# One crossbar transpose per token tile in place of two, in an attention kernel followed by a two-layer network

## Chip, cores, metric

One core of a Trainium2 chip. The metric is the device time of the kernel in microseconds, median of several executions. "PE" is TensorE, "DVE" VectorE, "ACT" ScalarE, "POOL" GpSimd and "SP" SyncE in the profile.

## The reference

```python
# q, k, v: (4 batches, 8 heads, 768 positions, 64); three of the heads are "retrieval" heads
scores = q @ k.T / 8
mask   = causal, and for the other heads: 4 sink positions or a window of 64
a      = softmax(scores masked);  attn = a @ v
x      = attn as (3072 tokens, 512)
h      = x @ w_in                # 512 -> 2048
out    = (h - tanh(h)) @ w_out   # 2048 -> 512, float32
```

## The kernel before

Tokens are worked on in 12 tiles of 256 (two blocks of 128, `NB = 2`). A small scheduler in Python (`Plan`) gets every operation with an assumed duration, its inputs and outputs, plays the engines through, and emits the instructions in the order that it finds. From tile 3 on ("ranked" tiles) the attention output `x16t` of a tile is transposed by DMA into `xT`; in tiles 0 to 2 PE transposes it and DVE or ACT copies it into `xT`. The first layer then reads `xT`:

```python
def st_X_tile(t):
    xTs[t] = lazy(xt_pool, [128, HP, TT], FP16, "xT", f"xT{t}")      # HP = 4, TT = 256
    for i in range(NB):
        op("SP", 1250,                                               # assumed ns of issue
           lambda i=i: nc.sync.dma_start_transpose(
               out=xTs[t]()[:, :, i * 128 : i * 128 + 128],
               in_=x16s[t]()[:, i, :, :].rearrange("p h d -> p (h d)")),
           r=[("x16t", t)], w=[("xT", t, "all", i)], dma=(512, 22.0))  # packets, ns each
# ... first layer of a tile, two blocks of 128 features a unit
nc.tensor.matmul(out=ph()[:, j, :], lhsT=w()[:, cb, c0 + fb % 4 : c0 + 512 : 4],
                 rhs=xTs[t]()[:, cb, :], start=(cb == 0), stop=(cb == HP - 1))
# ... a finished block of 128 tokens is stored
op(ring, 420, lambda: engs[ring].dma_start(out=out[t0:t0+128, c0:c1], in_=ot()[:, c0:c1]), ...)
# ... the whole is followed by a branch to a second version of the program, not taken with these inputs
program(True)
with tc.If(many[0] > NGEN, preferred_fallthrough_block=True, label="redo"):
    program(False)
```

SyncE issues nearly all loads of q, k and v, all transposes by DMA and all stores but one. Each of its transfers, when it has landed, signals a semaphore (a counter on which an engine can wait).

The softmax here doesn't subtract the row's maximum and nothing guards it: scores larger than these inputs give would overflow.

Of the kernel before, what the change touches and what calls it, by code (L numbers as in the profile page):

```python
# [8 lines left out]
FP16 = mybir.dt.float16  # L9
# [3 lines left out]
TT = 256  # L13
NB = TT // 128


class Plan:
# [42 lines left out]
    def run(self, fill=None, until=None):  # L60
        self.fill = fill
        n = len(self.ops)
        users = [[] for _ in range(n)]
        followers = [[] for _ in range(n)]
        left = [0] * n
        for i, o in enumerate(self.ops):
            left[i] = len(o[3]) + (o[7] is not None)
            for d in o[3]:
                users[d].append(i)
            if o[7] is not None:  # L70
                followers[o[7]].append(i)
        ready = [0.0] * n
        free = dict.fromkeys(self.ENGINES, 800.0)
        queue = {e: [] for e in self.ENGINES}
        rings = {"SP": [], "POOL": []}
        now = 0.0
        self.start = [0.0] * n
        self.done = [0.0] * n
        order = []

        self.port = 0.0

        def at(i):

            return max(ready[i], self.port) if self.ops[i][6] else ready[i]

        def enqueue(i):
            queue[self.ops[i][0]].append(i)

        def finish(i, done):  # L90
            self.done[i] = done
            e, ns = self.ops[i][:2]
            for u in users[i]:
                to = self.ops[u][0]
                if to == e and e == "PE":
                    at = self.start[i] + ns
                else:
                    at = done + (60 if to == "PE" else 40)
                ready[u] = max(ready[u], at)
                left[u] -= 1  # L100
                if not left[u]:
                    enqueue(u)

        for i in range(n):
            if not left[i]:
                enqueue(i)
        while len(order) < n:
            t, e = min(
                [(max(free[e], min(at(i) for i in q)), e) for e, q in queue.items() if q],
                default=(1e12, None),  # L110
            )

            live = [r for r in rings.values() if r and r[0][1] <= now]
            nxt = min([r[0][1] for r in rings.values() if r and r[0][1] > now], default=1e12)
            if live:
                pk = sum(r[0][2] for r in live)
                end, r = min((now + r[0][3] * pk / r[0][2], k) for k, r in enumerate(live))
                stop = min(end, nxt, t)
                for x in live:
                    x[0][3] -= (stop - now) * x[0][2] / pk  # L120
                now = stop
                if end <= min(nxt, t):
                    i = live[r].pop(0)[0]
                    finish(i, now + 1300)
                    continue
                if nxt < t:
                    continue
            elif nxt < t:
                now = nxt
                continue  # L130
            now = max(now, t)
            i = min(
                (i for i in queue[e] if at(i) <= t), key=lambda i: self.ops[i][5]
            )
            queue[e].remove(i)
            _, ns, _, _, dma, _, port, _ = self.ops[i]
            if e == "PE" and t < 5600:
                ns *= 2
            self.start[i] = t
            order.append(i)  # L140
            free[e] = t + max(ns - self.OVERLAP[e], 40)
            if port:
                self.port = free[e]
            for u in followers[i]:
                ready[u] = max(ready[u], free[e])
                left[u] -= 1
                if not left[u]:
                    enqueue(u)
            if dma:
                packets, each = dma  # L150
                rings["POOL" if e == "POOL" else "SP"].append(
                    [i, t + ns + (1200 if e == "POOL" else 1000 if t < 6000 else 400), each, packets * each / 16]
                )
            else:
                finish(i, t + ns + self.RESULT[e])
        self.end = max(self.done)
        free = self.FROM
        for i in order:
            if self.ops[i][0] == "PE":
                idle = self.start[i] - free  # L160
                if self.fill and idle > 200 and i != until and self.FROM < free:
                    self.fill(int(idle * 0.5 / 107), 256)
                free = max(free, self.start[i] + self.ops[i][1])
                if i == until:
                    self.fill = None
            self.ops[i][2]()
# [3 lines left out]
def kernel(  # L170
# [98 lines left out]
    def program(first):  # L269
# [19 lines left out]
        def lazy(pl, shape, dt, tag, name):  # L289
            box = []  # L290

            def get():
                if not box:
                    box.append(pl.tile(shape, dt, tag=tag, name=name))
                return box[0]

            return get
# [813 lines left out]

        def st_X_tile(t):

            xTs[t] = lazy(xt_pool, [128, HP, TT], FP16, "xT", f"xT{t}")
            for i in range(NB):
                op(
                    "SP", 1250,
                    lambda i=i: nc.sync.dma_start_transpose(
                        out=xTs[t]()[:, :, i * 128 : i * 128 + 128],
                        in_=x16s[t]()[:, i, :, :].rearrange("p h d -> p (h d)"),  # L1120
                    ),
                    r=[("x16t", t)], w=[("xT", t, "all", i)], dma=(512, 22.0),
                )

        def x_keys(t):
            if ranked(t):
                return [("xT", t, "all", i) for i in range(NB)]
            return [("xT", t, c) for c in range(HP)]

        def st_X(n, tag="m", eng="DVE"):  # L1130
            t, hp = divmod(n, HP)
            if hp == 0:
                xTs[t] = lazy(xt_pool, [128, HP, TT], FP16, "xT", f"xT{t}")
            xp, key = bank([128, NB, 128], FP16, tag, f"xp{n}")

            def mm():
                for i in range(NB):
                    nc.tensor.transpose(
                        out=xp()[:, i, :], in_=x16s[-1 - n]()[:, i, :, :], identity=ident16[:]
                    )  # L1140

            first_x.append(op("PE", 112, mm, r=[("x16", n), "ident"], w=[key]))
            op(
                eng, {"ACT": 373, "DVE": 290}[eng],
                lambda: copy(eng, xTs[t]()[:, hp, :], xp()[:].rearrange("p i c -> p (i c)")),
                r=[key], w=[("xT", t, hp)],
            )

# [6 lines left out]
        def H_unit(t, u):  # L1155
            if u == 0:
                gts[t] = lazy(g_pool, [128, NFB, TT], FP16, "gt", f"gt{t}")
            ph, key = bank([128, FU, TT], FP32, "h", f"ph{t}_{u}")
            for j in range(FU):

                def mm(j=j):
                    fb = u * FU + j
                    w, c0 = w_in_t[fb // 4]
                    for cb in range(HP):
                        nc.tensor.matmul(  # L1165
                            out=ph()[:, j, :], lhsT=w()[:, cb, c0 + fb % 4 : c0 + 512 : 4],
                            rhs=xTs[t]()[:, cb, :], start=(cb == 0), stop=(cb == HP - 1),
                        )

                op(  # L1170
                    "PE", 4 * 109, mm,
                    r=[("win", u * FU // 4)] + x_keys(t), w=[key],
                )
            th = lazy(th_pool, [128, FU, TT], FP32, "th", f"th{t}_{u}")
            tk = ("th", t * NFU + u)
            op(
                "ACT", 597,
                lambda: nc.scalar.activation(  # L1178
                    out=th()[:], in_=ph()[:], func=AF.Tanh, scale=1.0 / XS
                ),  # L1180
                r=[key], w=[tk],
            )
            op(
                "DVE", 687,
                lambda: nc.vector.scalar_tensor_tensor(  # L1185
                    out=gts[t]()[:, u * FU : (u + 1) * FU, :], in0=th()[:], scalar=-XS,
                    in1=ph()[:], op0=ALU.mult, op1=ALU.add,
                ),
                r=[key, tk], w=[("gt", t, u)],
            )  # L1190
# [287 lines left out]
```

## Time and profile before

| | before |
|---|---|
| median (runs) | 237.61 us (237.30 to 237.75) |
| span of the profiled execution | 235.8 us |
| PE busy, 80 to 230 us | 150.0 of 150 us |
| start of the last matmul, from the trace | 229.84 us |
| transfers issued by SyncE, from the trace | 127 |

The rows are from two views of the kernel before, SyncE's instructions of line 1441 (the end of the branch) and of line 1473 (the end of the program); the columns are least, median and greatest duration in ns, then the first and the last start in us.

```profile
L1441 SPq EVENT_SEMAPHORE  x8: 17/17/17, 233.0 to 233.5; - x8
...
L1473 SPq EVENT_SEMAPHORE  x14: 17/28/28, 233.6 to 235.7; - x14
L1473 SPq DRAIN  x3: 7/7/136, 234.8 to 235.2; - x3
```

Eight waits, one for each of the semaphores of its transfers, stand one after the other and take 17 ns each; but each starts 0.07 to 0.1 us after the one before. They begin at 233.0 us, when the last store has landed, and only when all eight are through does the closing sequence of line 1473 begin.

### The profile page before, as it was taken

The numbers are of one execution on the slowest core, as the hardware profiler recorded it, in microseconds if no ns is written. First come the engines' busy times: TensorE is split into PE (matmuls) and PEld (weight loads), VectorE is DVE, ScalarE is ACT, GpSimd is POOL, SyncE is SP. The second block draws the span as 40 slices with busy tenths as digits, with TensorE's granted clock in tenths as the row PEclk, the third lists the DMA queues.
The fourth block names the chain that finished last, engine by engine and source line by source line (L and its number), as shares of the span: only waits on it lengthen the run. The fifth ranks groups of instructions, "written<-read, shape, count | busy, mean of one in ns | idle before, by whom it ended". The sixth has DMA issues, their size and how long they took to land. (4 is left out here: it accounts for less than half of the span.)

```text
span 235.8 us, 5930 instructions
## 1 busy us (share of the span) xinstructions
PE 223.4 (95%) x2234; PEld 158.4 (67%) x2234; DVE 138.9 (59%) x343; ACT 143.2 (61%) x221; POOL 90.2 (38%) x218
## 2 busy tenths in 40 slices
PE   6888899999999999999999999999999999999990
PEld 2455687766675787677777767767677677777660
DVE  3657667862688468658675647567576555434400
ACT  3886749883676498547668458456856754444410
POOL 5798250198709087570904829144000000000000
PEclk9999999999999999999999999999999999999997
DMA  5999999999899999979998995987302101410021
GB/s 129 266 199 207 194 187 219 216 244 204 111 220 189 230 232 184 232 175 191 204 193 199 181 230 121 200 187 141 86 3 81 37 19 47 90 44 26 21 101 41
DMA packets 106084, 35.83 MB, mean 152 GB/s; under 512 B 96195, under 2 KB 102595, under 8 KB 106051
## 3 DMA queue, kind: packets, MB, share of 16 engines
q1 hardware_dynamic: 94754, 30.03, 62.6%
q0 software_dynamic: 11008, 5.24, 16.8%
q8 instruction: 18, 0.29, 0.6%
q10 hardware_dynamic: 288, 0.14, 0.2%
q14 instruction: 16, 0.12, 0.2%
HBM read 27.27 MB, written 6.29 MB: 142 GB/s over the span
## 5 line engine op out<-in xcount | busy, mean ns | idle before, releaser
L1165 PE MATMUL ph<-xT,win 128*128 128x256 f16 x768 | 100.7, 273 | 1.6 <-DMA win<-in_moe_w_in_dram 0.6
L1224 PE MATMUL po<-wout,gt 128*128 128x512 f16 (+1 forms) x400 | 97.4, 371 | 0.3 <-ACT ot L1200 0.3
L1185 DVE SCALAR_TENSOR_TENSOR gt<-th,ph 128x512 f16<-128x512 f32 x96 | 65.6, 685 | 50.1 <-ACT th L1178 49.6
L1178 ACT ACTIVATE th<-ph 128x512 f32<-128x512 f32 x96 | 57.6, 601 | 60.8 <-PE ph L1165 56.4
L1165 PEld LDWEIGHTS <-win 128*128 128x128 f16 x768 | 80.6, 114 | 14.4 <-issue 2.2
L991 ACT ACTIVATE pt<-sc 128x1024 f16<-128x1024 f32 (+1 forms) x78 | 68.6, 927 | 8.8 <-PE sc L971 8.5
L1224 PEld LDWEIGHTS <-gt 128*128 128x128 f16 x400 | 36.4, 98 | 25.5 <-issue 1.0
L709 POOL CAST t<-raw_rqk 128x256 f16 x72 | 28.9, 439 | 56.1 <-DMA raw_rqk<-in_k_dram 47.6
L1060 PEld LDWEIGHTS <-pt 128*128 128x128 f16 x552 | 25.1, 97 | 9.8 <-DVE pt L1021 0.7
L1060 PE MATMUL av<-v,pt 128*128 128x65 f16 x304 | 25.5, 193 | 0.2 <-DVE pt L1021 0.2
L704 POOL CAST v<-raw_rv 128x128 f16 x72 | 21.8, 335 | 4.0 <-DMA raw_rv<-in_v_dram 4.0
L971 PE MATMUL sc<-qk 64*128 64x128 f16 (+1 forms) x412 | 23.1, 236 | 0.0
L1090 DVE TENSOR_TENSOR x16t<-av,rinv 128x128 f32 x72 | 20.8, 289 | 2.0 <-DVE rinv L1080 0.2
L1200 ACT ACTIVATE ot<-po 128x512 f32<-128x512 f32 (+1 forms) x24 | 14.3, 594 | 10.7 <-PE po L1224 10.0
L971 PEld LDWEIGHTS <-qk 64*128 64x128 f16 x412 | 13.6, 94 | 9.7 <-issue 6.7
L1060 PE MATMUL av<-vf,pt 128*128 128x65 f16 x248 | 19.6, 193 | 0.0
L1080 DVE RECIPROCAL rinv<-av 128x4 f32<-128x4 f32 x48 | 8.6, 179 | 11.3 <-PE av L1060 11.1
L1016 DVE TENSOR_TENSOR pt<-pt,mS 128x512 f16<-128x512 f16 x24 | 10.4, 473 | 7.7 <-ACT pt L991 7.7
L1026 DVE TENSOR_TENSOR pt<-pt,m 128x1024 f16<-128x1024 f16 x16 | 11.8, 737 | 4.4 <-ACT pt L991 4.4
L780 POOL TENSOR_TENSOR vf<-v,rflagr 128x260 f16<-128x260 f16 x12 | 7.7, 643 | 0.0
L872 PEld LDWEIGHTS <-t 128*128 128x128 f16 x48 | 3.2, 97 | 5.9 <-ACT t L673 2.4
L459 PE MATMUL warm<-ones 128*128 128x512 f16 (+1 forms) x14 | 4.7, 487 | 1.2 <-POOL ones L454 1.2
(98 smaller groups left out, 95.4 us busy)
## 6 DMA issues: line engine op xcount, KB each, us to landing
out_dram<-ot SPq DMA_DIRECT2D x23, 256.0 KB, 2.8
raw_rqk<-in_q_dram SPq DMA_DIRECT2D x22, 256.0 KB, 4.8
raw_rqk<-in_k_dram SPq DMA_DIRECT2D x22, 256.0 KB, 4.7
raw_rv<-in_v_dram SPq DMA_DIRECT2D x18, 256.0 KB, 5.0
win<-in_moe_w_in_dram POOLq DMA_DIRECT2D x4, 512.0 KB, 9.8
wout<-in_moe_w_out_dram POOLq DMA_DIRECT2D x4, 512.0 KB, 11.7
raw_rv<-in_v_dram SPq DMA_DIRECT2D x4, 128.0 KB, 4.7
v<-in_v_dram POOLq DMA_DIRECT2D x4, 128.0 KB, 9.3
```

Source lines behind the costliest of these rows:

```text
L704: nc.gpsimd.tensor_copy(out=v1s[b]()[:, lo : lo + NB, rank : rank + 1, 0:D], in_=raw_of("v", t)[:, :, at, :],)
L709: nc.gpsimd.tensor_copy(out=t16[t % 2][:, :, :, rank : rank + 1, :], in_=raws["rqk", t][0]()[:, :, :, at, :],)
L971: nc.tensor.matmul(out=sc()[:, hh, o : o + nb * 128].rearrange("p (i c) -> p i c", c=128), lhsT=ks.rearrange("p i c -> p (i c)")[p_, jb * ...
L991: lambda pt=pt, gi=gi, wid=wid, sc=sc: nc.scalar.activation(out=pt()[:, :, 512 * gi : 512 * gi + wid], in_=sc()[:, :, 0:wid], func=AF.Exp, ...
L1026: nc.vector.tensor_mul(out=pv, in0=pv, in1=m4[:, h0 : h0 + 2, 256:512].unsqueeze(2).to_broadcast([128, 2, 2, 256]),)
L1060: nc.tensor.matmul(out=av()[:, i, hh, :], lhsT=pt()[:, hh, co : co + 128], rhs=vv, start=(jb == first_jb), stop=(jb == qb),)
L1090: nc.vector.tensor_mul(out=x16s[t]()[:, :, at, :], in0=av()[:, :, hh : hh + 1, 0:D], in1=rinv()[:, :, hh : hh + 1].unsqueeze(3).to_broadca ...
L1165: nc.tensor.matmul(out=ph()[:, j, :], lhsT=w()[:, cb, c0 + fb % 4 : c0 + 512 : 4], rhs=xTs[t]()[:, cb, :], start=(cb == 0), stop=(cb == HP ...
L1178: lambda: nc.scalar.activation(out=th()[:], in_=ph()[:], func=AF.Tanh, scale=1.0 / XS),
L1185: lambda: nc.vector.scalar_tensor_tensor(out=gts[t]()[:, u * FU : (u + 1) * FU, :], in0=th()[:], scalar=-XS, in1=ph()[:], op0=ALU.mult, op ...
L1200: nc.scalar.activation(out=ot()[:, c0:c1], in_=po()[:, c0:c1], func=AF.Copy, scale=1.0 / XS)
L1224: nc.tensor.matmul(out=po()[:, c0:c1], lhsT=gts[t]()[:, f, ts * 128 : ts * 128 + 128], rhs=w_out_t[f // 4]()[:, f % 4, c0:c1], start=(f == ...
```

## The change

The intent: one transfer of 1024 columns a tile in place of two of 512, so nine transfers fewer in SyncE's queue. For that `xT` lies in order of token blocks, and its readers and writers follow.

```diff
-            xTs[t] = lazy(xt_pool, [128, HP, TT], FP16, "xT", f"xT{t}")
-            for i in range(NB):
-                op("SP", 1250,
-                    lambda i=i: nc.sync.dma_start_transpose(
-                        out=xTs[t]()[:, :, i * 128 : i * 128 + 128],
-                        in_=x16s[t]()[:, i, :, :].rearrange("p h d -> p (h d)")),
-                    r=[("x16t", t)], w=[("xT", t, "all", i)], dma=(512, 22.0))
+            xTs[t] = lazy(xt_pool, [128, NB, HP, 128], FP16, "xT", f"xT{t}")
+            op("SP", 1250,
+                lambda: nc.sync.dma_start_transpose(
+                    out=xTs[t]()[:].rearrange("p i c k -> p (i c) k"),
+                    in_=x16s[t]()[:].rearrange("p i h d -> p (i h d)")),
+                r=[("x16t", t)], w=[("xT", t, "all")], dma=(1024, 22.0))
 ... tiles 0 to 2
-                lambda: copy(eng, xTs[t]()[:, hp, :], xp()[:].rearrange("p i c -> p (i c)")),
+                lambda: copy(eng, xTs[t]()[:, :, hp, :], xp()[:]),
 ... first layer
-                            out=ph()[:, j, :], ...
-                            rhs=xTs[t]()[:, cb, :], ...
+                            out=ph()[:, j, :].rearrange("p (i k) -> p i k", i=NB), ...
+                            rhs=xTs[t]()[:, :, cb, :], ...
```

(Lines are joined. Left out are the list of keys for which the readers of `xT` wait, which follows the change, and a rewriting of one assumed latency that leaves its value as it was.)

More of the change, by code (lines that the diff above doesn't have):

```diff
@@ L151, in run @@
                 rings["POOL" if e == "POOL" else "SP"].append(
-                    [i, t + ns + (1200 if e == "POOL" else 1000 if t < 6000 else 400), each, packets * each / 16]
+                    [i, t + ns + (1200 if e == "POOL" and t < 12000 else 1200 if e == "POOL" else 1000 if t < 6000 else 400), each, packets * each / 16]
                 )
@@ L1112, in st_X_tile @@
         def st_X_tile(t):
-            xTs[t] = lazy(xt_pool, [128, HP, TT], FP16, "xT", f"xT{t}")
-            for i in range(NB):
-                op(
-                    "SP", 1250,
-                    lambda i=i: nc.sync.dma_start_transpose(
-                        out=xTs[t]()[:, :, i * 128 : i * 128 + 128],
-                        in_=x16s[t]()[:, i, :, :].rearrange("p h d -> p (h d)"),
-                    ),
-                    r=[("x16t", t)], w=[("xT", t, "all", i)], dma=(512, 22.0),
-                )
+            xTs[t] = lazy(xt_pool, [128, NB, HP, 128], FP16, "xT", f"xT{t}")
+            op(
+                "SP", 1250,
+                lambda: nc.sync.dma_start_transpose(
+                    out=xTs[t]()[:].rearrange("p i c k -> p (i c) k"),
+                    in_=x16s[t]()[:].rearrange("p i h d -> p (i h d)"),
+                ),
+                r=[("x16t", t)], w=[("xT", t, "all")], dma=(1024, 22.0),
+            )
         def x_keys(t):
             if ranked(t):
-                return [("xT", t, "all", i) for i in range(NB)]
+                return [("xT", t, "all")]
             return [("xT", t, c) for c in range(HP)]
@@ L1132, in st_X @@
             if hp == 0:
-                xTs[t] = lazy(xt_pool, [128, HP, TT], FP16, "xT", f"xT{t}")
+                xTs[t] = lazy(xt_pool, [128, NB, HP, 128], FP16, "xT", f"xT{t}")
             xp, key = bank([128, NB, 128], FP16, tag, f"xp{n}")
@@ L1165, in mm @@
                         nc.tensor.matmul(
-                            out=ph()[:, j, :], lhsT=w()[:, cb, c0 + fb % 4 : c0 + 512 : 4],
-                            rhs=xTs[t]()[:, cb, :], start=(cb == 0), stop=(cb == HP - 1),
+                            out=ph()[:, j, :].rearrange("p (i k) -> p i k", i=NB),
+                            lhsT=w()[:, cb, c0 + fb % 4 : c0 + 512 : 4],
+                            rhs=xTs[t]()[:, :, cb, :], start=(cb == 0), stop=(cb == HP - 1),
                         )
```

## The prediction

> **What bounds the kernel now.** The median of three runs is 237.61 us (237.30 to 237.75); the profiled execution spans 235.8 us. I first read the busy shares and the 40 slices of the page.
>
> ```profile
> PE 223.4 (95%) x2234; PEld 158.4 (67%) x2234; DVE 138.9 (59%) x343; ACT 143.2 (61%) x221; POOL 90.2 (38%) x218
> ...
> PE   6888899999999999999999999999999999999990
> PEclk9999999999999999999999999999999999999997
> DMA  5999999999899999979998995987302101410021
> ```
>
> TensorE is busy in every slice but the first few and the last, at a full granted clock. The DMA engines are nearly full too, but only to slice 27 (about 160 us). Busy ends of matmuls are modelled, so I asked for the busy time by stretch.
>
> ```profile
> 0.00:40.00 40.00, 34.31 (x355) 23.04 (x356) 24.66 (x74) 27.67 (x48) 23.48 (x42) 1.00 1.29 198
> 40.00:80.00 40.00, 38.94 (x443) 26.96 (x441) 26.84 (x74) 26.55 (x40) 22.18 (x59) 1.00 1.17 203
> 80.00:230.00 150.00, 150.00 (x1442) 108.40 (x1439) 86.97 (x197) 88.97 (x134) 44.52 (x117) 1.00 0.60 131
> 230.00:236.00 6.00, 0.11 (x2) 0.00 (x0) 0.42 (x1) 0.00 (x0) 0.00 (x0) 0.76 0.10 33
> ```
>
> The columns after the length of the stretch are PE, weight load, VectorE, ScalarE and GpSimd. From 80 to 230 us PE has no idle time that the trace shows; before 40 us it has 5.7 us, between 40 and 80 us 1.1 us, and the tail of 6 us is the last store. To see hidden stalls I took the distances between the starts of neighbouring matmuls in the trace from 40 to 230 us. A matmul of the first layer (256 columns) is followed by its like after a median of 109 ns (577 cases, at most 138), one of 512 columns after 216 ns (272 cases, at most 228). So PE streams. What is left over those steps: each visit to the score matmuls costs 96 ns on entry (205 ns in place of 109 from a first-layer matmul) and about 95 ns on leaving (148 in place of 53). That is a fixed price of switching, about 31 visits, 5.9 us. True waits after 70 us I count as four, 1.4 us together. PE's own wait list from 60 us on is this:
>
> ```profile
> PE ph L1165 <- DMA xT<-x16t: 0.4, 1, 0.4
> PE po L1224 <- ACT ot L1200: 0.3, 1, 0.3
> PE av L1060 <- DVE pt L1021: 0.2, 1, 0.2
> ```
>
> One of them, once, is for the transposed x that the change touches. It is tile 3, the first that is transposed by DMA:
>
> ```profile
> 72.09 2.53 SPq L1118 DMA_TRANSPOSE xT<-x16t  x2
> 74.67 1.48 SPq L342 DMA_DIRECT2D raw_rqk<-in_k_dram  x1
> ...
> 77.35 0.22 PE L1060 MATMUL av<-v,pt 128*128 128x65 f16 x2
> 77.93 1.50 PE L1165 MATMUL ph<-xT,win 128*128 128x256 f16 x12 [0.36 <-DMA xT<-x16t]
> ```
>
> By the landing semaphores the two halves landed at 77.24 and 77.89 us, and the matmul began at 77.93. For the other eight tiles the second half landed ahead of the first matmul that reads it by 4.9, 1.9, 7.8, 10.7, 2.8, 10.8, 9.3 and 4.7 us (tiles 4 to 11, from the same semaphores and the matmuls' starts). So the transposes are off the critical path but for half a microsecond.
>
> **What the Trainium skill says.** (1) "DMA: Bandwidth & Descriptors", Rules for kernel authors: small transfers should be coalesced into large ones, and under Issuing engines are not separate DMA queues, all of them run on the same 16 engines, so issue is a sequencer cost. The trace agrees on the issue side: a transpose of half the size costs as much to issue. (2) Same page, Latency and other measured facts: a DMA transpose gets 261 GB/s with a non-contiguous middle dimension and about 350 to 400 GB/s contiguous. The new destination is contiguous within a partition, the old one is not; for 256 KB that is, as an estimate from this page, 1.0 against about 0.7 us. The trace can't confirm it: loads run beside the transposes. (3) "TensorE: Matmul & The Clock Gate", Back-to-back issue gap: 256 columns take 262 cycles and 512 take 518 when warm; the 109 and 216 ns above agree.
>
> **The change part by part.**
>
> ```profile
> L1118 SPq DMA_TRANSPOSE xT<-x16t x18: 1189/1244/3186, 72.1 to 201.3; - x18
> ...
> DMA to landing us min/median/max: 2.3/2.7/5.2
> ...
> L727 SPq DMA_TRANSPOSE qk<-t x18: 1244/1324/2774, 52.6 to 160.7; - x18
> ...
> DMA to landing us min/median/max: 3.0/3.8/5.0
> ```
>
> The numbers are least, median and greatest issue time in ns; the second pair are the transposes of q and k, which have just the size of the new one (128 partitions by 1024 columns, where the old one had 512).
>
> *Removed:* nine transposes. 18 issues by 1244 ns = 22.4 us of SyncE become nine of 1244 to 1324 ns = 11.2 to 11.9 us. SyncE's queue is 10.5 to 11.2 us shorter, 1.2 us a tile. No engine's busy time has it, and PE waits for SyncE in one place only, so on the path it is worth at most that wait.
>
> *Moved, the transposed x's arrival:* before, the second half is issued 1.24 us after the first and lands 2.7 us later, 3.9 us in all; after, one issue lands in 3.8 us (the q and k row). A saving of 0.1 us in the usual case, for eight tiles hidden behind at least 1.9 us. For tile 3 the rings were backlogged: the first half needed 5.15 us, and the second, issued 1.27 us later, came 0.65 us after it. Both were queued by 74.6 us, so the same packets should end at about the same 77.9 us; if the contiguous destination helps, 0.3 us sooner. Worth 0 to 0.3 us there, and never more than the stall: from the last attention matmul, which normally occupies 29 ns, to the first-layer one is 550 ns, so 0.5 us.
>
> *Moved, loads behind it:* each goes out about 1.2 us earlier up to 160 us. They feed GpSimd's casts, which wait for q and k in 34.2 us of the stretch after 60 us, and still PE waits for none of it. Off the path: 0.
>
> *Added, the layout that PE reads:* the 576 first-layer matmuls of the nine tiles, and the 192 of the three others, read 256 columns as two runs of 128 elements, 1 KB apart. If a run's end cost even 5 ns, 768 would be 3.8 us, the largest number in this sum. Against it: the mask matmuls already read two runs of 256 and follow each other after 215 ns, just like 512 contiguous columns (216); the score matmuls read 256 columns in two runs with gaps between them, at a 105 to 117 ns step where they are not paired. So I take 0.
>
> *Added, twelve copies into the new layout* for tiles 0 to 2: the copies into q and k's tile already write two runs of 128 with a gap, in 288 ns on VectorE against 289 for x, and 388 against 377 ns on ScalarE. At most 8 by 11 ns = 0.1 us, on engines that are not the bound.
>
> *Moved, the order of the program:* the kernel's instructions are ordered by a small scheduler in Python that assumes times. With one transpose it believes x to be ready earlier: issue 1250 + 400 + 1024 packets by 22 ns over 16 engines (1408) + 1300 = 4358 ns, where two gave 2500 + 400 + 704 + 1300 = 4904 ns. So from tile 3 on it may place first-layer matmuls up to 0.55 us earlier in PE's queue, and everything after can fall differently. The earlier part is unchanged.
>
> Sum on the path: tile 3's wait 0 to -0.5 us, mostly 0.2; layout 0; reordering of unknown sign, of the order of a half microsecond. That gives 237.6 - 0.2 = 237.4 us.
>
> **Rivals.** *Reordering makes new stalls.* For it: the believed gain of 0.55 us a tile is not real (0.1 us by the trace), so the wait of tile 3 can grow from 0.5 to 1.0 us. Against it: for the other tiles the believed 4.4 us still exceeds the usual 3.8. It would make 237.9 to 238.3 us. *Reordering helps:* if two visits to the score matmuls merge, 0.19 us each; three merged, with tile 3's wait gone, 236.5 us. All of the true waits after 70 us gone is 1.4 us: 236.2 us, about the floor. *PE pays for the two runs:* 5 ns each, 241.4 us, still only 1.6%; the mask matmuls speak against it. *SyncE was the bound after all:* 11 us fewer of issue would then show as several per cent, as the 47 us of GpSimd's waits for loads suggest; PE's 150 busy of 150 us speaks plainly against it.
>
> **Range and chances.** The runs before spread over 0.45 us. With -0.5 to +0.5 us of reordering on top of the central -0.2 us, 236.5 to 238.2 us should hold it 8 times in 10. Two per cent is 4.75 us, more than all true waits of PE after 40 us and more than the layout's cost at 5 ns a matmul, so within 2% gets 0.97; slower gets 0.02 for a layout cost that the mask matmuls don't show, faster 0.01.
>
> **What would show it.** Right: nine issues of x's transpose at 1.2 to 1.3 us, landing in 3 to 4 us; first-layer matmuls still 109 ns apart; PE still 150 busy in 150 us; PE's wait for the transposed x at most 1 us, once. Wrong: steps above 112 ns in the first layer (the layout costs); several PE waits for the transposed x (the scheduler was misled); an issue of over 2 us (one large transpose is no cheaper than two); or an end of PE's stream that moved by over 1.5 us with none of these, which would mean that the visits to the score matmuls changed in number.

## The result, and the profile after

| | before | after |
|---|---|---|
| median of 4 runs each | 237.46 us (237.10 to 237.75) | 236.14 us (236.09 to 236.29) |
| ratio | | 0.9946, interval 0.9929 to 0.9964 |
| span of the profiled execution | 235.8 us | 234.5 us |
| last matmul starts | 229.84 us | 229.41 us |
| last store landed | 232.98 us | 232.75 us |
| from its landing to the span's end | 2.78 us | 1.71 us |
| transfers issued by SyncE | 127 | 118 |

Ratios here and below are not quite the ratio of the medians quoted; the range in brackets after a ratio is its 95% interval.

It is within 2%, as forecast, but 0.36 us below the range. The page of the changed kernel, its slices and the stretches:

```profile
PE 223.7 (95%) x2234; PEld 158.4 (68%) x2234; DVE 138.5 (59%) x343; ACT 143.3 (61%) x221; POOL 87.6 (37%) x218
...
PE   7888899999999999999999999999999999999991
```

```profile
40.00:80.00 40.00, 39.14 (x445) 27.12 (x443) 27.09 (x75) 26.79 (x41) 22.11 (x59) 1.00 1.13 204
80.00:230.00 150.00, 149.68 (x1439) 108.17 (x1437) 86.50 (x197) 88.80 (x134) 42.07 (x117) 1.00 0.61 130
```

PE is as full as before (the missing 0.32 us lie after its last matmul). The first-layer matmuls, which now read two runs of 128, still follow each other after a median of 109 ns (581 cases from 40 to 230 us). PE's waits from 60 us on, the transposes and tile 3's first matmul of the changed kernel:

```profile
PE po L1224 <- ACT ot L1200: 0.3, 1, 0.3
PE ph L1164 <- DMA xT<-x16t: 0.2, 1, 0.2
PE av L1060 <- DVE pt L1021: 0.2, 1, 0.2
```

```profile
L1117 SPq DMA_TRANSPOSE xT<-x16t x9: 1232/1282/1532, 72.3 to 199.6; - x9
...
DMA to landing us min/median/max: 2.7/2.8/5.9
```

```profile
77.11 0.22 PE L1060 MATMUL av<-v,pt 128*128 128x65 f16 x2
77.54 1.14 PE L1164 MATMUL ph<-xT,win 128*128 128x256 f16 x9 [0.21 <-DMA xT<-x16t]
```

So the one wait that the change could touch went from 0.36 to 0.21 us of idle time, no more. The rest of the gain is not in PE's stream at all. SyncE's last instructions of the changed kernel, in the views shown of the kernel before:

```profile
L1441 SPq EVENT_SEMAPHORE  x8: 17/17/17, 231.2 to 232.8; - x8
...
L1473 SPq EVENT_SEMAPHORE  x14: 17/28/28, 232.8 to 234.4; - x14
L1473 SPq DRAIN  x3: 7/7/13, 233.6 to 233.9; - x3
```

Two things differ. The eight waits now start at 231.2 us, 1.6 us ahead of the last one, and the closing sequence begins as soon as the last is through. And the first of the three drains takes 13 ns in place of 136, and comes 0.79 us after the end of the waits where it came 1.20 us after.

The trace tells why the waits differ. SyncE always waits for its semaphores in the order 100, 101, 104, 105, 106, 107, 108, 109. Before, the last store signalled semaphore 100, the first in that order: SyncE stood there until 232.98 us, then still had to go through seven more. After, with nine transfers fewer, the turn has moved on, and the last store signals 109, the last in the order: seven waits were over when it landed. The sum of the profiled pair is 0.43 us (last matmul) - 0.20 us (the last store took 3.34 in place of 3.14 us from the last matmul's start to its landing; it took 3.13 to 3.52 us over all profiles) + 1.07 us (landing to end) = 1.30 us, the difference of the spans.

### The profile page after: what moved, and what is told of

Read it like the earlier page. It is cut to its first block, busy times and chain, and to the rows that moved or that the text cites. A ratio compares the mean times of both kernels' runs of the same rounds, so it can differ in the third digit from the quotient of the medians. Undisturbed runs are those within 1.5% of the kernel's fastest.

```text
span 234.5 us, 5919 instructions
## 1 busy us (share of the span) xinstructions
PE 223.7 (95%) x2234; PEld 158.4 (68%) x2234; DVE 138.5 (59%) x343; ACT 143.3 (61%) x221; POOL 87.6 (37%) x218
## 5 line engine op out<-in xcount | busy, mean ns | idle before, releaser
L709 POOL CAST t<-raw_rqk 128x256 f16 x72 | 27.4, 420 | 56.3 <-DMA raw_rqk<-in_k_dram 31.1
L704 POOL CAST v<-raw_rv 128x128 f16 x72 | 20.1, 316 | 6.0 <-DMA raw_rv<-in_v_dram 6.0
L459 PE MATMUL warm<-ones 128*128 128x512 f16 (+1 forms) x14 | 5.2, 528 | 1.2 <-POOL ones L454 1.2
```

Source lines behind the costliest of these rows:

```text
L704: nc.gpsimd.tensor_copy(out=v1s[b]()[:, lo : lo + NB, rank : rank + 1, 0:D], in_=raw_of("v", t)[:, :, at, :],)
L709: nc.gpsimd.tensor_copy(out=t16[t % 2][:, :, :, rank : rank + 1, :], in_=raws["rqk", t][0]()[:, :, :, at, :],)
```

## The experiments

The theory is that the gain has three parts: PE's stream, the semaphore of the last store, and the pause ahead of the closing drain. Rivals: the new order of the instructions gives it; the single large transfer gives it; or the end differs by chance. e1 to e4 ran together (before: median 237.62 us), then e5 to e7 (before: 238.04 us), both groups on chip 14, and then e8 to e11 on chip 10 (before: 237.47 us). All results were correct.

**e1_order_only: the new order, but two transfers in the old layout.**

```diff
+            def turn():
+                for i in range(NB):
+                    nc.sync.dma_start_transpose(... as before ...)
+            op("SP", 1250, turn, r=[("x16t", t)], w=[("xT", t, "all")], dma=(1024, 22.0))
```

> Still two transposes per tile into the old layout, but the scheduler plans them as one, so every engine's order is that of the changed kernel. Theory (the 1.3 us are three parts: 0.43 us in PE's stream, about 0.5 us because the last store's semaphore is no longer the first of the eight that SyncE waits for at the end, about 0.4 us at SyncE's closing drain): the number of SyncE transfers is unchanged at 127, so the end stays as before (the last store on semaphore 100, waits after its landing 0.53 us); only what reordering gives of the 0.43 us can show: 237.0 to 237.5 us, ratio 0.998 to 1.000. Rival (reordering alone gave the gain): 236.1 us, ratio 0.9945.

Measured 237.67 us (237.39 to 239.02), ratio 1.0002 (0.9988 to 1.0016). The orders were compared instruction by instruction and are those of the changed kernel. The reordering alone gives nothing. The profiled execution happened to be the slowest of the seven (239.02 us, granted clock 0.988), yet its end fits: semaphore 100, 2.70 us from landing to end.

**e2_merge_old_order: one transfer in the new layout, but every engine's order as before.**

```diff
             for i in range(NB):
-                op("SP", 1250, lambda i=i: ... half a tile ...,
+                op("SP", 1250, (turn, lambda: None)[i],        # turn issues the one large transfer
                    r=[("x16t", t)], w=[("xT", t, "all", i)], dma=(512, 22.0))
```

> One transpose per tile into the new layout, but planned as two, so every engine's order is that of the kernel before. Theory: 118 SyncE transfers, the last store on semaphore 109, the last waited for, so the end is as short as after the change (from the start of the last matmul to the span's end 5.05 us in place of 5.92): 236.4 to 236.8 us, ratio 0.995 to 0.997. Rival (reordering alone): 237.5 us, ratio 1.000.

Measured 236.98 us (236.53 to 237.12), ratio 0.9972 (0.9958 to 0.9986). A gain is there without the new order, though 0.2 us short of the 236.8 expected at most. It is half of the first pair's (ratio 0.9946), but near the 0.9965 that the changed kernel itself shows in e10 below. The last store is on 109, and landing to end is 1.70 us.

**e3_before_plus7: the kernel before and seven useless transfers more.** This is the sharpest test: only the count of transfers changes, and in the wrong direction for any theory that likes fewer of them.

```diff
+                if first and t == NTT - 2 and ts == 1:       # after the store of tile 10
+                    for p in pads:                           # seven tiles of one element
+                        nc.sync.dma_start(out=p[:], in_=ones[0:1, 0:1])
```

> The kernel before with seven transfers of one element more on SyncE, issued at about 210 us where its queue is idle; nothing else. 134 transfers put the last store on semaphore 109 as after the change. Theory: PE's stream as before (its last matmul starts at 229.8), but the seven waits of 0.53 us now run before the store lands: 236.5 to 237.0 us, ratio 0.996 to 0.998. Rival (the end differs by chance, or for fewer transfers as such): 237.5 us or more, ratio 1.000 or above.

Measured 236.61 us (236.31 to 238.95); two of six runs had a granted clock of 0.991 and were long, so the ratio is 0.9982 with a wide interval, 0.9949 to 1.0016. (The transfers went out at 224 us, not 210, and pushed the last but one store from 227.3 to 228.3 us; the last store was not delayed.) Its end is that of the changed kernel, here as 1.70 us from landing to end:

```profile
L1476 SPq EVENT_SEMAPHORE  x14: 17/28/28, 233.1 to 234.6; - x14
L1476 SPq DRAIN  x3: 7/7/13, 233.8 to 234.1; - x3
...
L1444 SPq EVENT_SEMAPHORE  x8: 17/17/17, 231.4 to 233.0; - x8
```

**e4_before_plus8: one useless transfer more than e3.**

> As e3_before_plus7 with eight transfers more: 135, the last store back on semaphore 100. Theory: the seven waits come after the landing again, 237.4 to 237.6 us, ratio 1.000; against e3_before_plus7 one tiny transfer more costs 0.5 us or more. If the closing drain depends on how many instructions SyncE has run, its 0.4 us may be gone here: 237.1 us. Rival (no effect of the semaphore): the same time as e3_before_plus7 within 0.1 us.

Measured 237.59 us (237.20 to 239.39), ratio 1.0009 (0.9981 to 1.0037): one transfer of one element costs 1.0 us of median against e3. In its profile the waits begin at 233.5 us again, after the landing, and landing to end is 2.24 us:

```profile
L1476 SPq DRAIN  x3: 7/7/13, 234.9 to 235.2; - x3
...
L1444 SPq EVENT_SEMAPHORE  x8: 17/17/17, 233.5 to 234.1; - x8
```

So 0.54 us of the 1.0 are the semaphore. The drain is short here although the last store is on 100: the two effects are separate. With the pause gone I had 237.1 us down, and the median doesn't show that; in this profile the last matmul started at 230.06 us, the latest of the undisturbed profiles, and the eight transfers ran just ahead of the last two stores.

**e5_after_plus1 and e6_after_plus8: the same on the changed kernel**, with one and eight useless transfers.

> The changed kernel with one transfer of one element more on SyncE at about 210 us, so 119 transfers and the last store on semaphore 100, the first that is waited for. Theory: PE's stream as in the changed kernel (last matmul starts at 229.4 us), the seven waits after the landing again: 236.6 to 237.1 us, ratio to before 0.996 to 0.998, that is 0.5 to 0.9 us over the changed kernel. Rival (the merge itself gives the gain): 236.1 us, ratio 0.9945.

> The changed kernel with eight tiny transfers more: 126, the last store on semaphore 109 as in the changed kernel. Theory: 236.1 to 236.3 us, ratio 0.9945, faster than e5_after_plus1 in spite of seven transfers more. If the closing drain depends on SyncE's number of instructions, up to 0.4 us more. Rival (fewer transfers as such give the gain): slower than e5_after_plus1.

Measured 237.58 us (236.93 to 239.13), ratio 0.9986 (0.9948 to 1.0024), and 237.24 us (236.85 to 238.48), ratio 0.9969 (0.9934 to 1.0004). Both are above what I expected. Of the runs made together here, the kernel before, e5 and e6 each had some at a clock of 0.987 to 0.990, so these intervals decide nothing, and the 0.3 us between the two are within them. The profiles do: e5 is on semaphore 100 without the pause, 2.25 us from landing to end; e6 is on 109 with the pause (a drain of 136 ns), 2.23 us. I expected e6 to end sooner than e5; it doesn't, because the pause that I had allowed for came and used up the gain.

**e7_layout_only: two transfers in the old order, into the new layout.**

```diff
-                        out=xTs[t]()[:, :, i * 128 : i * 128 + 128],
+                        out=xTs[t]()[:, i, :, :],
```

> Two transposes per tile as before and in the order of before, but into the new layout, so each half is contiguous and the first layer reads two runs. Theory: the layout costs PE nothing (steps of 109 ns), 127 transfers and the last store on semaphore 100: 237.3 to 237.6 us, ratio 0.999 to 1.000; tile 3's first-layer matmul may come up to 0.2 us earlier if the contiguous destination lands sooner. Rival (contiguity gives the gain of the stream): last matmul at 229.4 us in place of 229.8, 237.1 us.

Measured 237.80 us (237.55 to 238.40), ratio 0.9989 (0.9958 to 1.0020). First-layer steps of 109 ns, last matmul at 229.75 us, semaphore 100, landing to end 2.78 us just as in the kernel before. No cost or gain of the layout shows.

**The pause.** In all kernels with a pause (before, e1, e6, e7) the trace has a gap of 0.40 to 0.41 us, where 0.07 is usual, and it stands ahead of the same instruction, the 200th recorded one of SyncE: in the kernel before that is the drain, in e1, with one instruction more ahead of it, the wait before the drain. The changed kernel, e2 and e5 have 195 to 197 instructions in all and end before it. But e3 and e4 pass it without a gap. They wait for the store 6 and 12 instructions ahead of it, the others 13 to 20. Two kernels were made to test both rules at once, by the count of the useless transfers alone:

> The kernel before with three tiny transfers more: 130, the last store on semaphore 105, the fourth of eight in the order of the waits. Read from the profile, from the store's landing to the span's end. Theory: four waits of 0.07 us come after the landing (1.70 + 0.28 us); the pause of 0.4 to 0.5 us that the kernel before, e1, e6 and e7 show at the same instruction of SyncE's stream (its 200th recorded one) is there again, since SyncE waits for the store 14 instructions ahead of it: 2.4 to 2.55 us. Rival 1 (the semaphore acts as a switch, not one wait at a time): 1.7 or 2.2 us. Rival 2 (the pause comes by chance): 1.95 to 2.05 us.

> As e8_before_plus3 with four transfers: 131, the last store on semaphore 106, the fifth. Theory: three waits after the landing (1.70 + 0.21 us), and no pause, since SyncE now waits for the store 12 instructions ahead of its 200th one, as in e4, where none was seen: 1.85 to 1.95 us from landing to end, that is 0.5 to 0.6 us less than e8_before_plus3 for one transfer more. Rival (the pause needs a certain number of instructions alone, whatever SyncE waits for): as e8, 2.35 to 2.5 us.

Measured from landing to end: 2.42 and 1.90 us, both inside what the theory said, and outside what each rival said. In e8 (semaphore 105, fourth) the gap of 0.40 us is ahead of the 200th instruction; in e9 (106, fifth) it is gone. Times: e9 236.66 us (two runs, ratio 0.9964), e8 237.77 us (two runs of 237.0 and 238.54 us, too few to say more). SyncE's waits in e9 and e8, in this order:

```profile
L1444 SPq EVENT_SEMAPHORE  x8: 17/17/17, 231.2 to 233.1; - x8
```

```profile
L1444 SPq EVENT_SEMAPHORE  x8: 17/17/17, 233.0 to 234.7; - x8
```

Their last matmuls started at 229.40 and 231.28 us (e8's profile fell in the long run), so in both the waits begin some 1.75 us after it and the last one is through 0.2 to 0.3 us after the landing (232.92 and 234.40 us): three and four waits were left.

All ends, in us from the last store's landing to the span's end, from the traces:

| | semaphore 100 (first) | 105, 106 | semaphore 109 (last) |
|---|---|---|---|
| with the pause | 2.78 (before), 2.78 (e7), 2.70 (e1) | 2.42 (e8) | 2.23 (e6) |
| without | 2.24 (e4), 2.25 (e5) | 1.90 (e9) | 1.71 (after, e10), 1.70 (e2, e3, e11) |

Thirteen ends, and each is 1.70 us + about 0.07 to 0.08 us for each wait left + some 0.5 us (0.44 in e8) for the pause.

**e10_after_again and e11_before_plus7_again: the two kernels at equal ends, on one chip.**

> The changed kernel as it is, on the same chip as e11, to compare the two at equal ends: 118 transfers, last store on semaphore 109, landing to end 1.7 us. Theory: 0.9 to 1.3 us under the kernel before, and 0.1 to 0.4 us under e11 (what the merge gives in PE's stream, chiefly tile 3). Rival (the merge gives nothing in the stream): as e11 within 0.1 us.

> e3 again, for comparison with e10 on one chip: two transposes per tile and seven tiny transfers, landing to end 1.7 us. Theory: 0.8 to 1.1 us under the kernel before, 0.1 to 0.4 us over e10. Rival: as e10.

Measured 236.40 us (236.18 to 237.49), ratio 0.9965 (0.9949 to 0.9980), and 236.41 us (236.30 to 236.56), ratio 0.9956 (0.9943 to 0.9968). The rival won: with the end made alike, two transposes a tile are as fast as one. Over the undisturbed profiles the last matmul started at 229.40 to 230.06 us with two transposes (mean 229.68, six profiles) and at 229.41 to 229.69 us with one (mean 229.54, five). So the 0.43 us of the first pair is mostly scatter of the stream; what the merge gives there is 0.1 us or nothing, and these runs can't tell which.

No version was found that beats both kernels: e11 and the changed kernel are equal.

## Why the prediction was wrong, and where it was right

**Wrong: the end of the program.** The step that failed is the one headed *Removed*: "No engine's busy time has it, and PE waits for SyncE in one place only, so on the path it is worth at most that wait." It followed from an earlier half sentence, "the tail of 6 us is the last store", which I had not looked into. The 5.9 us after the last matmul's start are in the kernel before 0.82 us to the store's issue, 2.32 us to its landing, and 2.78 us of SyncE working through its own list. The nine transfers were worth 1.07 us there, not by their time but by their number: the store's place in the turn of eight semaphores (0.53 us) and where in SyncE's stream the pause fell (0.54 us). The sum on the path lacked this term; with it, -0.2 - 1.07 us gives 236.3 us for the 237.61 I started from.

**Right: transposes off the path.** Nine issues with a median of 1.28 us (I had 1.24 to 1.32), 12.0 us together for 24.2 before, and PE waited for the transposed x once, as said. The usual landing after 2.8 us was earlier than the 3.8 us I took over from q and k's transposes, which run where loads are dense; hidden either way.

**Right: tile 3.** I gave it 0 to 0.3 us. From the first issue to the last landing it took 5.27 us on the mean of eight profiles with two transfers (4.84 to 5.82) and 5.27 us on the mean of five with one (5.01 to 5.58). Both halves do wait in the same backlog.

**Right: the layout.** 109 ns a step, and copies of 372 and 292 ns (medians after) as before.

**Harmless: the order.** I allowed a half microsecond either way; e1 shows 1.0002, and e2 and e11 gain without it. The rival of misled placement did not come true: tile 3's wait did not grow.

**A reading that was wrong, without effect on the result.** Of the four waits of 1.4 us that I counted "after 70 us", one, of 0.37 us, is at 64.0 us; after 70 us there are three, 1.0 us together. The floor of 236.2 us in the rival *Reordering helps* rests on the four.

**Not settled: the pause.** Its place and the condition are shown in thirteen profiles, one of each run (the 200th instruction, unless SyncE waits for the last store within 12 instructions ahead of it), not its cause. That it is SyncE's instruction stream being fetched is an argument, and one that fits: a fixed place in the stream, and a long wait close ahead of it that hides it. The Trainium skill, "Runtime: NRT & Kernel Launch", Instruction fetch mechanics, says that a sequencer fetches the next page by DMA while it executes the current one, that crossing a boundary is "mostly hidden", and that a taken branch whose target lies outside the current window of two pages breaks this sequential prefetch; SyncE has just jumped over the second program. But no packet of the queues that carry instructions lies in the gap in the kernel before (nearest starts at 232.13 and 235.38 us, the gap is at 234.34), nor in that of e1, e6, e7 or e8, so the traces don't show it. Two things are left out of this argument. The kernel marks a hint for this very branch (`expect_skip`), and the trace has a BRANCH_PREFETCH_HINT of SyncE at 0.8 us. And the pause stands at the same count in the kernel before and in e6, although the second program that is jumped over has nine transposes fewer in e6: if it lies between the branch and the end, a boundary at a fixed address would have moved. A rival that no run tests is that the profiler itself makes the pause after a number of records.

## What to carry to other kernels

When the busiest engine streams without gaps, the next thing to read is what comes after its last instruction: the tail is on the critical path in full, and here a change that touched nothing in it moved it by 1 us through the count of transfers. A gain of a half per cent from a change in the middle of a kernel should be traced to a place before it is credited to the mechanism; padding the old kernel with useless transfers (e3, e11) gave the same gain. And a scatter of 0.4 us in the stream from one profile to the next is enough to fake a part of it, so compare several profiles before giving a stretch its share.

## What the Trainium skill lacked or had wrong

- "DMA: Bandwidth & Descriptors" (Queues, rings and completion order) tells of completion semaphores but not that a program may wait for them one by one at its end, in a fixed order, so that the last transfer's place in the turn counts: 1.70 us from landing to end with the last place, 2.24 us with the first, both without the pause: 0.08 us for each of seven waits.
- "Runtime: NRT & Kernel Launch" (Instruction fetch mechanics) calls the crossing of a block mostly hidden and warns of a stall after a taken branch, but gives no time for it. If the pause is of that kind, which is not shown, it was a gap of 0.40 us in place of 0.07, and about 0.5 us of the kernel's time, in five of thirteen profiles.
- "DMA: Bandwidth & Descriptors" (Rules for kernel authors) advises to coalesce small transfers. Where another engine is the bound and the transfers are hidden, this gave no time: 236.40 us with one transfer a tile, 236.41 us with two and an equal end. (The halves are of 128 KB, and so not among those under 64 KB that the page warns of.)
- The same page (Latency and other measured facts) has a faster figure for a contiguous transpose and doesn't say of which side. The prediction took it for the destination's, and no run shows it there: from issue to landing a half took at least 2.30 us into the old layout (before) and 2.31 us into the contiguous one (e7), and tile 3, in a backlog of loads, took 5.27 us with two transfers and with one.
